# Pooled V by GpSimd and the band mask added in PSUM, from pair 16 on: an hourglass attention with a dense layer behind it

## The chip, the cores and the metric

The kernel runs on one core of a Trainium2 chip. The metric is the device time of one execution in microseconds. The core has five engines that work side by side, each with its own instruction queue: TensorE (PE in the profile) multiplies matrices, VectorE (DVE), ScalarE (ACT) and GpSimd (POOL) work element by element, and SyncE (SP) issues nearly all DMAs here. Sixteen DMA engines move the data. An instruction waits in its queue until what it depends on is done, and everything behind it on that queue waits with it.

## The reference

Two parts follow each other. The first is attention over q, k and v of shape (8, 8, 576, 64): eight batches, eight heads, 576 tokens, 64 channels. Each head is computed twice and the results are added: once on tokens averaged in groups of four (144 of them, the result repeated four times), and once with a band mask that lets a token see only those less than four positions away.

```python
q_d = q.reshape(B, H, Sd, factor, D).mean(axis=3)      # factor = 4, Sd = 144; k_d, v_d likewise
out_up = np.repeat(sm_attn(q_d, k_d, v_d), factor, axis=2)
mask = np.abs(pos[:, None] - pos[None, :]) < factor
scores = np.where(mask, scale * np.matmul(q, k.transpose(0, 1, 3, 2)), -1000000000.0)
out_local = np.matmul(softmax(scores), v)
return out_up + out_local
```

The second part is dense, over x, the attention's result as 4608 tokens of 512 channels, with weights of 512 x 2048 and 2048 x 512:

```python
h = x @ w_in
g = h - np.tanh(h)
return g @ w_out
```

## The kernel before

**Tiling of attention.** Two heads of one batch make a pair; there are 32 pairs, four to a batch, and two pairs make a head block (`hb`). For the band, the 576 tokens are cut into five windows (`NT`) of 128 keys each, 112 apart, so a window's keys stand on the 128 partitions and its 112 or 120 queries on the free dimension. The pooled attention has 144 keys and queries (`G`). They are laid out window by window as well, 32 to a window, 160 columns in all (`GW`), with some groups in two windows.

**One pair, step by step.** SP loads q and k (`qkn`) and v (`vst`, in the window layout) in 64-channel fp32 rows. A cast to bf16 gives `qr` (line 452) and `vw` (line 390). A transpose, on TensorE for the first eight pairs and by DMA after that (line 457), gives channels on partitions, reordered by ScalarE into `qk` (line 465). Two additions (lines 499 and 508) sum each four neighbouring tokens into `qkd`. The scores are written into PSUM: the first four windows by line 517 into one pair of banks, the fifth window and the pooled scores (line 539) into another. From pair 14 on both go in one step, `s12`. ScalarE takes the exponentials into the tile `E`: line 557 the 912 columns of the first four windows, line 569 the 240 of the fifth, line 572 the 640 of the pooled scores. The band mask is then multiplied in: the large mask (912 columns, line 561) on VectorE, the small one (240 columns, line 576) on VectorE or GpSimd. The first four pairs (`BIASED`) instead get a bias from a matmul with the identity ahead of the scores. The output matmuls (lines 585 and 591) multiply `E` with `vw` and with the pooled v, `vd`, each of which has a column of ones (or fours) that gives the softmax sum. VectorE divides (lines 602 and 604) into `ln`. The result is transposed, by TensorE for pairs 0 to 7, 11 and 15 (lines 615 and 618), by a DMA for the other 22 (line 621, tile `lT`), and the pooled part, repeated four times, is added in the join (lines 633 and 637, on GpSimd or VectorE), which writes `xT`, the input of the dense part.

**Pooled v.** `pool_v(hb)` makes `vd` for two pairs at once: four matmuls with 32 columns of a pooling matrix (line 405) and one with 128 (line 407), then a copy out of PSUM (line 412), by ScalarE but for the first head blocks.

**The dense part.** Block `kb` of the dense part covers 512 tokens (even `kb`) or 640 (odd). Line 675 multiplies by `w_in` into PSUM (four matmuls for each of 16 slices of the hidden dimension, twice for an odd block), ScalarE takes tanh (line 686), VectorE subtracts (line 689) into `gT`, and line 711 multiplies by `w_out`. `dense(kb)` interleaves the first product of block `kb` with the second one of block `kb - 1`. Block `kb` can start when the joins of batch `kb` are done.

**The order.** The whole program is written as a list of operations with a duration, the keys they read and write, and a priority; some have alternatives on several engines (`P.choice`). `Program.order` then simulates the engines and issues at each moment the ready operation of lowest priority number. Attention's priorities are ten times the pair's number, the dense matmuls have 5000, so the dense part fills what attention leaves of TensorE. The simulated order is the order in each engine's queue on the chip. DMAs are simulated as one resource with a cost each (`T_QK`, `T_V`, `T_IN`, `T_OUT`), at most eight outstanding from SP. From pair 12 on (`GATE`) the loads of pair `p` wait until pair `p - 5`'s result was sent to its DMA transpose. Loads are issued four pairs ahead: there are four `qkn` and five `vst` buffers.

Of the kernel before, what the change touches and what calls it, by code (L numbers as in the profile page):

```python
# [8 lines left out]
FP32 = mybir.dt.float32  # L9
BF16 = mybir.dt.bfloat16  # L10
# [155 lines left out]
def kernel(  # L166
# [9 lines left out]
    nc = tc.nc  # L176
# [13 lines left out]
    PIECES = [(0, 0, 120), (1, 0, 112), (2, 0, 56), (2, 56, 56), (3, 0, 112), (4, 0, 120)]  # L190
    GW = 32 * NT
    Q0 = [0, 120, 232, 344, 456]
# [18 lines left out]
    bias = fixed("bias", [128, 576], BF16)  # L211
    xT = [fixed(f"xT{j}", [128, NTOK], BF16) for j in range(NP)]
    w_in_sb = fixed("w_in_sb", [128, N_DC, Dff], BF16)
# [136 lines left out]
    def load_v(p):  # L350

        b, j, s = p // NP, p % NP, p % NVST
        for i in range(2):
            queue = nc.scalar if p in V_ACT else nc.sync

            def issue(i=i, base=v[b, 2 * j + i], queue=queue):
# [4 lines left out]
                 [("sent", p - BEHIND)] if p in GATE else [])  # L361

    def load_w(src, dst, name, f, stage, keys):
# [32 lines left out]
    def pool_v(hb):  # L396

        w = hb % NVW
        pri = 20 * hb - 1
        bank, keys = (ps_ox1, ["ox1"]) if MERGE[2 * hb] else (ps_ox, ["ox"])  # L400
        pv = bank[:, 0, :].rearrange("p (w c) -> p w c", w=2)
# [17 lines left out]
    def attention(p):  # L419
# [7 lines left out]
        cold = 1.1 if p < NP else 1.0  # L427
        biased = p < BIASED


# [71 lines left out]
        def add2(eng):  # L502
            with nc.allow_low_precision("pooled q and k"):
                out = qkd[s].rearrange("p i (t r) -> p i t r", t=NT)
# [3 lines left out]
                eng.tensor_tensor(out=out, in0=a, in1=c, op=ALU.add)  # L508
# [20 lines left out]
        def s2(bank=ps):  # L529
# [6 lines left out]
            for i in range(2):  # L536
                for hh in range(2):
                    rows = slice(64 * hh, 64 * hh + 64)
                    T.matmul(bank[:, hh, 120 + GW * i:120 + GW * i + GW],  # L539
                             qkd[s][rows, 1, 32 * i:32 * i + 128],  # L540
                             qkd[s][rows, 0], start=True, stop=True)

# [13 lines left out]
        e3 = E[s][:, 1152:1792].rearrange("p (h c) -> p h c", h=2)  # L556
        op("ACT", 820, lambda: A.activation(  # L557
            out=e1, in_=ps[:, :, 0:456], func=AF.Exp, scale=SCALE),
           reads=ts, writes=[("E", s, 0)], pri=pri)
        if not biased:  # L560
            P.choice([(eng, ns, lambda fn=fn: fn(  # L561
# [4 lines left out]
        if not merged:  # L566
# [5 lines left out]
        op("ACT", 590, lambda: A.activation(  # L572
            out=e3, in_=ps2[:, :, 120:120 + 2 * GW], func=AF.Exp, scale=SCALE / 16.0),
           reads=ts2, writes=[("E", s, 2)], pri=pri)
        if not biased:
            P.choice([(eng, ns, lambda fn=fn: fn(  # L576
                out=e2v, in0=e2v, in1=mask[:, 456:576].unsqueeze(1).to_broadcast([128, 2, 120]),
                op=ALU.mult)) for eng, ns, fn in MASK2[p >= SMALL]],
                reads=["mask"], writes=[("E", s, 1)], pri=pri)

        def outs():
            for hh in range(2):
# [4 lines left out]
                for half in range(2):  # L587
                    c = 1152 + 2 * GW * hh + 128 * half
# [9 lines left out]
        op("PE", 590 * cold, outs,  # L598
           reads=[("E", s, 0), ("E", s, 1), ("E", s, 2), ("vw", w, jj), ("vd", w)],
           writes=ox, pri=pri)  # L600
# [19 lines left out]
        if XOUT[p] == 'dma':  # L620
# [7 lines left out]
            def join(eng):  # L628
                x = xT[j][:, b * S:(b + 1) * S]
                x0, p0 = (bass.AP(tensor=a.tensor, offset=a.offset,  # L630
                                  ap=[a.ap[0], [n, 2], [1, m]])
                          for a, n, m in ((x, 456, 120), (pool, 130, 30)))
                eng.tensor_tensor(
# [5 lines left out]
                    in0=lT[s][:, 1:4, 0:112].rearrange("p t (g a) -> p t g a", a=4),  # L639
                    in1=pool[:, 32:128].rearrange("p (t g) -> p t g", t=3)[:, :, 2:30]  # L640
                    .unsqueeze(3).to_broadcast([128, 3, 28, 4]), op=ALU.add)
# [93 lines left out]
    def dense(kb):  # L735
# [6 lines left out]
        for _, second, i in steps:  # L742
            if second:
                mm2(kb - 1, i)
            else:
# [155 lines left out]
```

## Time and profile before

| | us |
| --- | --- |
| Median of 3 runs | 327.32 (327.27 to 329.07) |
| The profiled execution, its own time | 327.29 |
| Its span, first to last instruction | 325.6 |

The span's 1.7 us of difference to the execution's time lie around it. The profile names instructions by engine, line of the kernel, and output and input tiles; a group's line gives the count, the busy time, the mean of one, and the idle time of the engine ahead of it with what ended it. In the windows, each engine's busy time in a stretch stands with the number of its instructions; after them the granted TensorE clock, the mean busy share of the sixteen DMA engines (packets overlap, so it can exceed 1) and GB/s. PEld is the loading of weights, which overlaps the matmuls.

### The profile page before, as it was taken

The page shows a single profiled execution, that of the slowest core. Times are in us where ns is not written, and L with a number is a line of the kernel's source. Part 1 is how long each engine was busy: PE and PEld are TensorE (multiplying, and loading weights), DVE is VectorE, ACT ScalarE, POOL GpSimd, SP SyncE. Part 2 cuts the span into 40 slices and gives each one's busy share as a digit, 9 for nine tenths or more (in the row PEclk, how much of TensorE's full clock was granted, in tenths as well). Part 3 has the DMA queues.
Part 4 walks back from the last instruction along what each step waited for, and adds up shares of the span by engine and source line. Part 5 has one row for each costly group of instructions (what it writes and reads, how often), then busy time and mean ns, then how long its engine had stood idle before and what let it go on. Part 6 is the DMA issues. An engine that isn't in the chain of part 4 may idle for free.

```text
span 325.6 us, 7167 instructions
## 1 busy us (share of the span) xinstructions
PE 313.9 (96%) x2643; PEld 175.5 (54%) x2686; DVE 212.5 (65%) x388; ACT 224.7 (69%) x390; POOL 165.6 (51%) x230
## 2 busy tenths in 40 slices
PE   6899999999899999999999999999999999999996
PEld 2565555666544445666654444656554445566544
DVE  6898985789966576765867576778665444554311
ACT  3765987599888969799986978798973444544300
POOL 5688758265846767677767767877440000000000
PEclk9999999999999999999999999999999999999999
DMA  7999999899987999699999999995322001000022
GB/s 205 316 393 367 372 315 273 216 259 217 240 254 106 254 201 294 92 234 219 191 233 165 261 209 263 222 229 106 85 66 62 32 32 67 32 34 32 32 84 81
DMA packets 109715, 59.79 MB, mean 184 GB/s; under 512 B 92656, under 2 KB 92912, under 8 KB 109680
## 3 DMA queue, kind: packets, MB, share of 16 engines
q1 hardware_dynamic: 109680, 59.33, 72.9%
q8 instruction: 21, 0.34, 0.5%
q14 instruction: 14, 0.11, 0.1%
HBM read 37.75 MB, written 9.44 MB: 145 GB/s over the span
## 4 chain that ended last, share of the span: by engine, by line
PE 90%; DVE 4%; issue 2%; POOL 1%; DMA 1%; ACT 1%; SPq 0%; POOLq 0%
PE ps_hy L711 38%; PE ps_hy L675 36%; PE ps_ox L517 3%; PE ps_ox L585 3%; PE ps_ox L591 2%; PE ps_ox L539 1%; PE ps_ox L405 1%; PE ps_ox L618 1%; PE ps_ox L407 1%; DVE ln L604 1%; DVE gT L689 1%; DMA qkn<-in_k_dram 1%; PE ps_ox L615 1%; PE ps_ox L482 1%; PE ps_ts L482 1%
## 5 line engine op out<-in xcount | busy, mean ns | idle before, releaser
L675 PE MATMUL ps_hy<-xT,w_in_sb 128*128 128x320 bf16 (+1 forms) x759 | 146.9, 325 | 1.7 <-DVE gT L689 1.0
L711 PE MATMUL ps_hy<-w_out_sb,gT 128*128 128x512 bf16 (+1 forms) x559 | 139.0, 373 | 2.2 <-issue 1.0
L689 DVE TENSOR_TENSOR gT<-ps_hy,u 128x320 bf16<-128x320 f32 (+1 forms) x192 | 103.2, 553 | 56.0 <-ACT u L686 53.1
L686 ACT ACTIVATE u<-ps_hy 128x320 f32<-128x320 f32 (+1 forms) x192 | 93.6, 497 | 53.2 <-PE ps_hy L675 47.3
L675 PEld LDWEIGHTS <-w_in_sb 128*128 128x128 bf16 x768 | 71.8, 98 | 53.4 <-issue 1.7
L711 PEld LDWEIGHTS <-gT 128*128 128x128 bf16 x592 | 56.0, 98 | 52.8
L499 POOL TENSOR_TENSOR half<-qk 128x576 f32<-128x576 bf16 x29 | 33.3, 1148 | 48.7 <-ACT qk L465 33.9
L465 ACT COPY qk<-qT 128x576 bf16<-128x576 bf16 x44 | 52.3, 1207 | 0.0
L452 POOL CAST qr<-qkn 128x576 bf16<-128x576 f32 x48 | 33.4, 707 | 13.0 <-DMA qkn<-in_k_dram 6.2
L604 DVE TENSOR_TENSOR ln<-ps_ox,r 128x896 bf16<-128x896 f32 x32 | 34.9, 1091 | 1.1
L561 DVE TENSOR_TENSOR E<-E,mask 128x912 bf16<-128x912 bf16 x28 | 24.0, 856 | 10.4 <-ACT E L557 10.4
L557 ACT ACTIVATE E<-ps_ox 128x912 bf16<-128x912 f32 x28 | 26.2, 937 | 4.9 <-PE ps_ox L517 4.6
L726 DVE COPY y<-ps_hy 128x512 f32<-128x512 f32 (+1 forms) x21 | 13.9, 663 | 20.2 <-PE ps_hy L711 19.1
L390 POOL CAST vw<-vst 128x640 bf16<-128x640 f32 x32 | 25.5, 796 | 2.4 <-DMA vst<-in_v_dram 2.3
L508 POOL TENSOR_TENSOR qkd<-half 128x320 bf16<-128x320 f32 x29 | 23.9, 823 | 1.8 <-DVE r L602 1.1
L572 ACT ACTIVATE E<-ps_ox 128x640 bf16<-128x640 f32 x28 | 20.0, 716 | 0.0
L585 PE MATMUL ps_ox<-vw,E 128*128 128x65 bf16 x320 | 19.3, 194 | 0.4 <-ACT vd L412 0.3
L585 PEld LDWEIGHTS <-E 128*128 128x128 bf16 x320 | 16.4, 98 | 5.7 <-issue 0.3
L576 POOL TENSOR_TENSOR E<-E,mask 128x240 bf16<-128x240 bf16 x18 | 13.6, 756 | 9.4 <-ACT E L569 9.3
L591 PE MATMUL ps_ox<-vd,E 128*128 128x65 bf16 x256 | 18.0, 193 | 0.1
L517 PEld LDWEIGHTS <-qk 64*128 64x128 bf16 x320 | 9.2, 95 | 16.1 <-issue 12.5
L602 DVE RECIPROCAL r<-ps_ox 128x14 f32<-128x14 f32 x32 | 7.7, 242 | 14.3 <-PE ps_ox L591 12.4
(78 smaller groups left out, 240.2 us busy)
## 6 DMA issues: line engine op xcount, KB each, us to landing
vst<-in_v_dram SPq DMA_DIRECT2D x64, 160.0 KB, 4.2
qkn<-in_q_dram SPq DMA_DIRECT2D x32, 288.0 KB, 4.1
qkn<-in_k_dram SPq DMA_DIRECT2D x32, 288.0 KB, 4.1
out_dram<-y SPq DMA_DIRECT2D x35, 256.0 KB, 2.5
gT<-in_moe_w_in_dram SPq DMA_DIRECT2D x4, 1024.0 KB, 8.1
xT<-in_moe_w_out_dram SPq DMA_DIRECT2D x8, 256.0 KB, 5.2
gT<-in_moe_w_out_dram SPq DMA_DIRECT2D x2, 1024.0 KB, 10.2
qT<-qr SPq DMA_TRANSPOSE x24, 4.2
```

The source lines that it names most:

```text
L390: P.choice([(eng, ns, lambda fn=fn: fn(out=vw[w][:, 2 * jj:2 * jj + 2, :, 0:64], in_=vst[s])) for eng, ns, fn in CAST_V[p >= NEARLY]], rea ...
L452: P.choice([(eng, ns, lambda dst=dst, srt=srt, fn=fn: fn(out=dst, in_=srt)) for eng, ns, fn in (any3[2:] if p >= CASTS else any3[:1] + any ...
L465: fn(out=full[:, i].rearrange("p (g a) -> p g a", a=A9), in_=qT[s][:, :, i::2].rearrange("p a g -> p g a"))
L499: eng.tensor_tensor(out=half, in0=four[:, :, :, 0:2], in1=four[:, :, :, 2:4], op=ALU.add)
L557: op("ACT", 820, lambda: A.activation(out=e1, in_=ps[:, :, 0:456], func=AF.Exp, scale=SCALE), reads=ts, writes=[("E", s, 0)], pri=pri)
L585: T.matmul(po[:, hh, 65 * t:65 * t + 65], E[s][:, c:c + 128], vw[w][:, 2 * jj + hh, t, :], start=True, stop=True)
L591: T.matmul(po[:, hh, o:o + 65], E[s][:, c + GW * i:c + GW * i + 128], vd[w][:, i, 2 * jj + hh, :], start=(i == 0), stop=(i == 1))
L604: op("DVE", 1010, lambda: V.tensor_tensor(out=ln[s].rearrange("p n (h d) -> p h n d", d=D), in0=blocks[:, :, :, 0:64], in1=r[s].unsqueeze( ...
L675: T.matmul(ps_hy[slot][:, 0:n], w_in_sb[:, dc, fc * 128:(fc + 1) * 128], xT[dc][:, t0 + c0:t0 + c0 + n], start=(dc == 0), stop=(dc == N_DC ...
L686: op("ACT", 90 + 76 * n // 100, lambda: A.activation(out=u[us][:, 0:n], in_=ps_hy[slot][:, 0:n], func=AF.Tanh), reads=[("hy", slot)], writ ...
L689: op("DVE", 70 + 105 * n // 100, lambda: V.tensor_tensor(out=gT[g][:, fc, c0:c0 + n], in0=ps_hy[slot][:, 0:n], in1=u[us][:, 0:n], op=ALU.s ...
L711: T.matmul(ps_hy[slot][:, 0:c1 - c0], gT[g][:, fc, ts * 128:ts * 128 + 128], w_out_sb[:, fc, c0:c1], start=(fc == 0), stop=(fc == N_FF - 1))
```

## The change

From pair 16 on (`DIRECT`), the pooled v of a pair no longer comes from `pool_v`. SP loads v a second time, in rows of four tokens (256 fp32 values) onto 72 partitions, two rows of each head to a partition (`load_pool`), into one of two buffers in the part of `xT` that belongs to batches 0 and 1. GpSimd sums the four tokens in two additions (`sum_v`). The pooled scores of these pairs use 144 columns in place of 160, and two tiles of 72 pooled keys in place of two of 128. Also from pair 16 on (`FORE`), VectorE adds the bias to the scores in PSUM ahead of the exponential, and the multiplication by the large mask behind it goes; the small mask stays a multiplication, on GpSimd only. From pair 8 on (`SMALL`, 12 before) the planner may put the small mask on GpSimd. Some durations that the planner is given change too.

```diff
-    xT = [fixed(f"xT{j}", [128, NTOK], BF16) for j in range(NP)]
+    xall = fixed("xT", [128, NP, NTOK], BF16)
+    xT = [xall[:, j] for j in range(NP)]
...
+    def load_pool(p):
+        b, j, n = p // NP, p % NP, p % 2
+        base = v[b, 2 * j]
+        def issue():
+            nc.sync.dma_start(out=vp(n), in_=bass.AP(
+                tensor=base.tensor, offset=base.offset,
+                ap=[[4 * D, KP], [KP * 4 * D, 4], [1, 4 * D]]))
+        load(650, issue, [("vp", n)] + [("x", c, i) for c in range(2) for i in range(NP)] * (p < DIRECT + 2),
+             T_P, -30 + 0.06 + 0.1 * p, behind=[("sent", p - BEHIND)])
+    def vp(n):
+        return xall[0:KP, :, 512 * n:512 * n + 512].bitcast(FP32)
+    def sum_v(p):
+        n, w, jj = p % 2, (p // 2) % NVW, p % 2
+        first = p < DIRECT + 2 * NVW
+        t = vp(n)
...
+        def add1(eng):
+            eng.tensor_tensor(out=t[:, :, 0:128], in0=t[:, :, 0:128],
+                              in1=t[:, :, 128:256], op=ALU.add)
+        def add2(eng):
+            with nc.allow_low_precision("pooled v"):
+                eng.tensor_tensor(out=vd[w][0:KP, jj, :, 0:64],
+                                  in0=t[:, :, 0:64], in1=t[:, :, 64:128], op=ALU.add)
+        for n1, fn, to in ((1030, add1, ("vp", n)), (630, add2, ("vdd", w, jj))):
+            P.choice([("POOL", n1, lambda fn=fn: fn(GP))],
+                     reads=[("vp", n)] + [("vd", w)] * first, writes=[to], pri=10 * p - 8)
...
+        if 2 * hb >= DIRECT:
+            return
...
-                    T.matmul(bank[:, hh, 120 + GW * i:120 + GW * i + GW],
-                             qkd[s][rows, 1, 32 * i:32 * i + 128],
-                             qkd[s][rows, 0], start=True, stop=True)
+                    k0 = (KP if direct else 32) * i
+                    T.matmul(bank[0:kp, hh, 120 + gw * i:120 + gw * i + gw],
+                             qkd[s][rows, 1, k0:k0 + kp],
+                             qkd[s][rows, 0, 0:gw], start=True, stop=True)
...
+        def add_bias(bank, part):
+            V.tensor_tensor(out=bank, in0=bank, op=ALU.add, in1=bias[:, part].unsqueeze(1)
+                            .to_broadcast([128, 2, part.stop - part.start]))
+        if p >= FORE:
+            op("DVE", 1025, lambda: add_bias(ps[:, :, 0:456], slice(0, 456)),
+               reads=["bias"], writes=ts, pri=pri)
...
-        if not biased:
+        if BIASED <= p < FORE:
...
-                op=ALU.mult)) for eng, ns, fn in MASK2[p >= SMALL]],
+                op=ALU.mult)) for eng, ns, fn in MASK2[p >= SMALL][p >= FORE:]],
...
-                                 E[s][:, c + GW * i:c + GW * i + 128],
+                                 E[s][0:kp, c + gw * i:c + gw * i + 128],
+                                 vd[w][0:kp, jj, 2 * hh + i, :] if direct else
...
+    FORE = 16
...
+    DIRECT, T_P = 16, 860
...
-    SMALL = 12
+    SMALL = 8
...
-    MASK1 = [[("DVE", 700, V.tensor_tensor)]] * 2
-    MASK2 = [[("DVE", 300, V.tensor_tensor)], [("DVE", 300, V.tensor_tensor), ("POOL", 700, GP.tensor_tensor)]]
+    MASK1 = [[("DVE", 760, V.tensor_tensor)]] * 2
+    MASK2 = [[("DVE", 300, V.tensor_tensor)], [("DVE", 300, V.tensor_tensor), ("POOL", 630, GP.tensor_tensor)]]
...
-    POOL_V = [("POOL", 670, GP.tensor_copy)]
+    POOL_V = [("POOL", 690, GP.tensor_copy)]
...
-            ("POOL", 610, GP.tensor_copy)]
+            ("POOL", 630, GP.tensor_copy)]
...
-    ADDERS = [[("DVE", 760, 450, V), ("POOL", 1100, 670, GP)],
-              [("POOL", 1100, 670, GP)]]
+    ADDERS = [[("DVE", 760, 450, V), ("POOL", 1120, 690, GP)],
+              [("POOL", 1120, 690, GP)]]
...
+            if nl[0] >= DIRECT:
+                load_pool(nl[0])
...
+            if p + 2 >= DIRECT:
+                sum_v(p + 2)
```

More of the change, by code (lines that the diff above doesn't have):

```diff
@@ L190 @@
     PIECES = [(0, 0, 120), (1, 0, 112), (2, 0, 56), (2, 56, 56), (3, 0, 112), (4, 0, 120)]
-    GW = 32 * NT
+    GW, KP = 32 * NT, G // 2
     Q0 = [0, 120, 232, 344, 456]
@@ L361, in load_v @@
                  [("sent", p - BEHIND)] if p in GATE else [])
+    def load_pool(p):
[13 more added lines that the diff above has]
+        t = vp(n)
+        if first:
+            op("DVE", 70, lambda: V.memset(vd[w][0:KP, jj, :, 64:65], 4.0),
+               writes=[("vd", w)], pri=10 * p - 12)
+        def add1(eng):
[8 more added lines that the diff above has]
+                     reads=[("vp", n)] + [("vd", w)] * first, writes=[to], pri=10 * p - 8)
     def load_w(src, dst, name, f, stage, keys):
@@ L428, in attention @@
         biased = p < BIASED
+        direct = p >= DIRECT
+        gw, kp = (G, KP) if direct else (GW, 128)
         yield
@@ L503, in add2 @@
             with nc.allow_low_precision("pooled q and k"):
+                if direct:
+                    eng.tensor_tensor(out=qkd[s][:, :, 0:G], in0=half[:, :, :, 0],
+                                      in1=half[:, :, :, 1], op=ALU.add)
+                    return
                 out = qkd[s].rearrange("p i (t r) -> p i t r", t=NT)
@@ L555, in attention @@
         e2v = E[s][:, 912:1152].rearrange("p (h c) -> p h c", h=2)
-        e3 = E[s][:, 1152:1792].rearrange("p (h c) -> p h c", h=2)
+        e3 = E[s][0:kp, 1152:1152 + 4 * gw].rearrange("p (h c) -> p h c", h=2)
+        def add_bias(bank, part):
[4 more added lines that the diff above has]
+               reads=["bias"], writes=ts, pri=pri)
         op("ACT", 820, lambda: A.activation(
@@ L572, in attention @@
         op("ACT", 590, lambda: A.activation(
-            out=e3, in_=ps2[:, :, 120:120 + 2 * GW], func=AF.Exp, scale=SCALE / 16.0),
+            out=e3, in_=ps2[0:kp, :, 120:120 + 2 * gw], func=AF.Exp, scale=SCALE / 16.0),
            reads=ts2, writes=[("E", s, 2)], pri=pri)
@@ L587, in outs @@
                 for half in range(2):
-                    c = 1152 + 2 * GW * hh + 128 * half
+                    c = 1152 + 2 * gw * hh + 128 * half
                     o = 65 * (NT + half)
@@ L598, in attention @@
         op("PE", 590 * cold, outs,
-           reads=[("E", s, 0), ("E", s, 1), ("E", s, 2), ("vw", w, jj), ("vd", w)],
+           reads=[("E", s, 0), ("E", s, 1), ("E", s, 2), ("vw", w, jj), ("vd", w)] +
+           [("vdd", w, jj)] * direct,
            writes=ox, pri=pri)
@@ L631, in join @@
                                   ap=[a.ap[0], [n, 2], [1, m]])
-                          for a, n, m in ((x, 456, 120), (pool, 130, 30)))
+                          for a, n, m in ((x, 456, 120), (pool, 114 if direct else 130, 30)))
                 eng.tensor_tensor(
@@ L639, in join @@
                     in0=lT[s][:, 1:4, 0:112].rearrange("p t (g a) -> p t g a", a=4),
-                    in1=pool[:, 32:128].rearrange("p (t g) -> p t g", t=3)[:, :, 2:30]
+                    in1=(pool[:, 30:114].rearrange("p (t g) -> p t g", t=3) if direct else
+                         pool[:, 32:128].rearrange("p (t g) -> p t g", t=3)[:, :, 2:30])
                     .unsqueeze(3).to_broadcast([128, 3, 28, 4]), op=ALU.add)
```

## The prediction, made before the changed kernel ran

> **What bounds the kernel now.** I read the page first, then the stages.
>
> ```profile
> span 325.6 us, 7167 instructions
> PE 313.9 (96%) x2643; PEld 175.5 (54%) x2686; DVE 212.5 (65%) x388; ACT 224.7 (69%) x390; POOL 165.6 (51%) x230
> ...
> PE   6899999999899999999999999999999999999996
> ...
> POOL 5688758265846767677767767877440000000000
> PEclk9999999999999999999999999999999999999999
> DMA  7999999899987999699999999995322001000022
> ...
> PE 90%; DVE 4%; issue 2%; POOL 1%; DMA 1%; ACT 1%; SPq 0%; POOLq 0%
> ```
>
> TensorE is busy in every slice but the first two and the last, at full granted clock, and the chain that ended last is 90% TensorE. The second thing to see is that the DMA engines are as full as TensorE for two thirds of the span, and empty in the last third. The windows split this by stage:
>
> ```profile
> core 0: us, PE busy (x) PEld busy (x) DVE busy (x) ACT busy (x) POOL busy (x), PEclk, DMA share, GB/s
> 0.00:27.00 27.00, 22.58 (x269) 13.34 (x272) 21.01 (x56) 14.16 (x22) 18.30 (x37) 1.00 0.97 310
> 110.00:220.00 110.00, 108.59 (x968) 60.45 (x985) 75.45 (x126) 91.63 (x151) 81.07 (x107) 1.00 1.02 217
> 247.00:325.60 78.60, 75.09 (x406) 40.26 (x411) 32.08 (x59) 26.86 (x55) 0.00 (x0) 1.00 0.14 50
> ```
>
> From 27 us on TensorE leaves almost nothing: attention's matmuls go first and dense ones fill in. So time can be won only by taking work off TensorE (or its few gaps), and lost only where attention becomes so late that the dense matmuls run out. Attention's own pace (pairs 16 to 31 lie mostly in the second row) has the DMA engines at a share of 1.02, ScalarE at 83%, GpSimd at 74%.
>
> ```profile
> 20.00:30.00 10.00, 9.43 (x117) 5.71 (x117) 8.46 (x13) 4.61 (x9) 8.66 (x15) 1.00 1.08 382
> 80.00:90.00 10.00, 9.12 (x110) 5.96 (x109) 9.89 (x20) 8.80 (x20) 7.50 (x11) 1.00 1.09 231
> 250.00:260.00 10.00, 9.95 (x47) 4.53 (x47) 4.19 (x7) 3.38 (x6) 0.00 (x0) 1.00 0.14 52
> ```
>
> The last row gives the price of a dense matmul of 512 columns: 47 in 10 us, 213 ns each, back to back.
>
> **The change, part by part.** First, pooling V on TensorE goes for head blocks 8 to 15.
>
> ```profile
> 152.29 0.81 PE L711 MATMUL ps_hy<-w_out_sb,gT 128*128 128x512 bf16 x3
> 153.03 0.29 PE L405 MATMUL ps_ox<-vw,pick 128*32 128x256 bf16 x4
> 153.26 0.29 PE L407 MATMUL ps_ox<-vw,pick 128*128 128x256 bf16 x1
> 153.38 1.25 PE L675 MATMUL ps_hy<-xT,w_in_sb 128*128 128x320 bf16 x8
> ```
>
> Three dense matmuls from 152.29 at 213 ns would hand over at 152.93; the next dense one starts at 153.38. The block costs 0.45 us: 0.35 in its five matmuls and 0.10 at its entry. The 64 matmuls of L405 below are 16 blocks, and eight go: 8 x 0.45 = 3.6 us off a full TensorE.
>
> ```profile
> L405 PE MATMUL ps_ox<-vw,pick 128*32 128x256 bf16 x64 | 4.7, 286 | 0.2 <-DVE xT L647 0.2
> L539 PE MATMUL ps_ox<-qkd 64*128 64x160 bf16 x112 | 8.4, 229 | 0.0
> L412 ACT CAST vd<-ps_ox 128x512 bf16<-128x512 f32 x15 | 8.9, 592 | 3.0 <-PE ps_ox L407 2.9
> L561 DVE TENSOR_TENSOR E<-E,mask 128x912 bf16<-128x912 bf16 x28 | 24.0, 856 | 10.4 <-ACT E L557 10.4
> L604 DVE TENSOR_TENSOR ln<-ps_ox,r 128x896 bf16<-128x896 f32 x32 | 34.9, 1091 | 1.1
> L576 POOL TENSOR_TENSOR E<-E,mask 128x240 bf16<-128x240 bf16 x18 | 13.6, 756 | 9.4 <-ACT E L569 9.3
> L499 POOL TENSOR_TENSOR half<-qk 128x576 f32<-128x576 bf16 x29 | 33.3, 1148 | 48.7 <-ACT qk L465 33.9
> ```
>
> The pooled scores narrow from 160 to 144 columns, four matmuls in each of 16 pairs: 64 x 16 columns at 213/512 ns is 0.4 us, half of that if the two halves of the rows run side by side. I take 0.2. The output matmuls keep their number and 65 columns, so nothing there.
>
> ScalarE loses eight copies of 592 ns and a tenth of its third exponential. It isn't the bound (83%), so this counts nothing, but it pays for what follows.
>
> The large mask becomes an addition in PSUM ahead of the exponential. The nearest row is L604, which also reads 896 fp32 elements from PSUM: 1.09 us, so about 1.1 against 0.86 for L561. On VectorE that is 16 x 0.25 = 4 us more at 69% busy. The chain of a pair stays as long but for that 0.25 us: score, add, exponential in place of score, exponential, mask. What is new is that ScalarE now waits for VectorE, with the tanh of the dense part queued behind it. A VectorE late by one L604 costs ScalarE about 1.1 us, against a spare of 18.4 us over some 14.7 pairs (110 us at about 7.5 a pair), 1.25 us a pair, and the 0.3 just freed. Cost 0; without that cover up to 1.1 us in some pairs. PSUM is held by the scores about 1.3 us longer of 7.5, and its other user there, the V pooling, is gone: 0.
>
> The small masks: 18 of the 20 from pair 12 on are on GpSimd already, so at most two move in the late pairs and four in pairs 8 to 11. Those four matter through the one gap that TensorE has after its start:
>
> ```profile
> 83.58 1.11 PE L675 MATMUL ps_hy<-xT,w_in_sb 128*128 128x320 bf16 x7 [0.78 <-DVE gT L689]
> ```
>
> In 80 to 90 us VectorE is busy 9.89 of 10, and TensorE waits 0.78 us for it. Less on VectorE there should close this: gain 0.8, bounds 0 and 0.8 (a new order of the whole program could also open one like it elsewhere, so 0.8 lost is the far end). The changed costs in the planner move work before pair 16 too; that has no row of its own, and I put it inside the same bound.
>
> GpSimd gets two additions per pair. By L499 (576 elements in 1148 ns, 2.0 ns each) 512 elements are 1.02 us and 256 are 0.5; together 1.5 a pair. It has 81.07/14.7 = 5.5 us of 7.5 now, so 7.0 to 7.2 with its masks: nearly full.
>
> ```profile
> L508 POOL TENSOR_TENSOR qkd<-half x29: 715/721/1208, 16.0 to 237.6; 128x320 bf16<-128x320 f32 x29
> L576 POOL TENSOR_TENSOR E<-E,mask x18: 637/641/1036, 98.1 to 243.3; 128x240 bf16<-128x240 bf16 x18
> ```
>
> ```profile
> 151.86 0.88 DVE L561 TENSOR_TENSOR E<-E,mask 128x912 bf16<-128x912 bf16 x1 [0.92 <-ACT E L557]
> ```
>
> ```profile
> 152.21 1.12 POOL L508 TENSOR_TENSOR qkd<-half 128x320 bf16<-128x320 f32 x1
> ```
>
> GpSimd's operations have a floor and a tail, and the tail case shown, 1.12 against 0.72 us, started under the mask multiplication L561. The Trainium skill, SBUF — State Buffer, section "SBUF: two separate sides", says that a VectorE operation with two SBUF inputs takes the port pair it shares with GpSimd exclusively for the whole instruction. The row agrees; by that rule the addition in PSUM, with one SBUF input, no longer blocks GpSimd, up to 0.4 us a pair back. No run shows it yet, and I leave it out of the sum; it lowers the chance of the GpSimd rival a little.
>
> The new load goes on SP's queue, among the q, k and V loads and both kinds of transposes, and waits for GpSimd to have read its buffer two pairs before. All transposes queue behind that wait.
>
> ```profile
> vst<-in_v_dram SPq DMA_DIRECT2D x64, 160.0 KB, 4.2
> qkn<-in_q_dram SPq DMA_DIRECT2D x32, 288.0 KB, 4.1
> ```
>
> It moves 72 x 4 x 256 fp32, 295 KB a pair, one q load's worth. Full DMA engines moved 382 GB/s at a share of 1.08 in 20 to 30 us (large pieces) and 217 at 1.02 in 110 to 220 us: 354 or 213 GB/s, 0.83 or 1.39 us a pair. Its 1 KB rows are nearer to the large pieces; I take 0.9. As the DMA engines are full, attention falls behind by that much a pair. Whether TensorE notices depends on the slack between a batch's last join and the first dense matmul that reads it:
>
> ```profile
> 0.00:163.70 163.70, 0.50 (x1) 6.92 (x9) 1.00 0.97 250
> ...
> 0.00:198.50 198.50, 1.44 (x2) 9.21 (x12) 1.00 0.99 245
> ...
> 0.00:255.00 255.00, 3.41 (x5) 13.05 (x17) 1.00 0.90 221
> ```
>
> ```profile
> 0.00:167.05 167.05, 72.59 (x379) 35.05 (x384) 1.00 0.97 251
> ...
> 0.00:204.01 204.01, 89.24 (x441) 41.09 (x448) 1.00 0.99 246
> ...
> 0.00:242.70 242.70, 110.41 (x569) 53.02 (x576) 1.00 0.93 228
> 242.70:273.50 30.80, 16.32 (x62) 6.20 (x64) 1.00 0.18 55
> ```
>
> The first fence counts joins (L637): 10, 14 and 22, with the ten pairs that TensorE turns back these are batches up to 4, 5 and 7. The second counts the weight loads of L675: even blocks have 64, odd ones 128, so 384, 448 and 640 end dense blocks 3, 4 and 6. Slack: 3.4 us for batch 4, 5.5 for batch 5, 18.5 for batch 7. The lateness would be 4 x 0.9 = 3.6, 8 x 0.9 = 7.2 and 14.4. When batch 5 is late, 16 matmuls of the dense block before it (4 x 4 x 213 ns = 3.4 us) can still go first, while a pair moved past that point takes its own matmuls away as cover (ten of about 115 columns, four of 144 and 18 of 65, 2,900 columns, 1.2 us at the same pace). So 7.2 + 1.2 - 5.5 - 3.4 is about zero, and 1.2 with half of the 16. I take 0.7 us lost.
>
> Sum: -3.6 - 0.2 - 0.8 + 0.7 = -3.9 us: a span of 321.7. The execution of that profile took 327.29, 1.7 beside its span, and the median shown is 327.32; so 323.4, say 323.5 us.
>
> **The rivals.** *The load is spread thin, slower than before.* It covers 72 partitions where the others cover 64 or 128. 72 does not split evenly over 16 engines as 64 and 128 do; over 12 it would, six partitions each, and those 12 would become the bound. Then the slow price is 1.39 x 16/12 = 1.85 us a pair. Batch 7 is then 16 x 1.85 = 29.6 late against 18.5 + 3.4, and some 2 us of cover are gone: 10 us idle, 327.3 - 4.6 + 10 = 332.7. It decides from 1.25 us a pair on (18.5 + 3.4 - 2 over 16 pairs; at batch 5 the first idle time comes at 0.96) and eats the whole gain at about 1.55. For it: the share of 1.02. Against it: each pair's loads start some four pairs ahead, and only slow pricing reaches it. The Trainium skill, DMA: Bandwidth & Descriptors, section "Why a DMA increments its semaphore by 16 and not by 1", gives the rule: the largest number up to 16 that divides the slowest dimension, here 12. No row shows a load of 72 partitions. With my 0.9 it would be 1.2 a pair: 9.6 + 1.2 - 5.5 - 3.4 = 1.9 idle, 327.3 - 4.6 + 1.9 = 324.6.
>
> *GpSimd becomes late, no change.* At 7.2 of 7.5 us an operation with the tail of L576 (0.4 us) in half to all of 16 pairs makes TensorE's output matmuls wait in order: 3 to 6 us, 326 to 329. For it: TensorE's order is fixed beforehand, so any lateness is a gap. Against it: the pace has slack as above, and the shared-port tail may shrink.
>
> *The order is only reshuffled.* If the gap at 83 us stays and the wait for batch 5 is 1.2, the sum is -2.6; with another gap of that size it is -1.8: 324.7 to 325.5. For it: every duration that the planner is given on GpSimd changes. Against it: the slack between attention and the dense blocks absorbs most of a changed order.
>
> **How the numbers follow.** One per cent, 3.3 us, is about what a measurement tells from no change: faster is below 324.0, slower above 330.6. Forecast with its gain kept, 0.50; the reshuffle and the milder DMA wait (324 to 326), 0.18; GpSimd late, 0.14; load spread thin, 0.18, nearly all of it above 330.6. The range starts at 321.5 (no wait at all and 1 us more off the start, where TensorE is busy 22.58 of 27) and reaches 331, which leaves most of the slow case out.
>
> **What would show it.** Right: L405 x32 in place of x64; TensorE's idle time as small as before from 27 us; no gap in 80 to 90 us; the PSUM addition near 1.1 us; GpSimd above 90% in 120 to 230 us; the end of attention some 10 us later with the dense blocks not waiting. Wrong: gaps of TensorE ahead of L675 that a join released (DMA), or ahead of L585 and L591 that GpSimd released; a landing of the new load far above 4.2 us; SP's queue waiting for GpSimd.

## The result, and the profile after

The changed kernel took 407.79 us (median of 6 runs, 403.88 to 411.50), the kernel before, run beside it, 327.35: a ratio of 1.243 (95% interval 1.237 to 1.249). The prediction was 323.5 us, with a range from 321.5 to 331.

The page of the changed kernel, with its busy times, TensorE's slices and granted clock, and the chain that ended last:

```profile
span 407.1 us, 7182 instructions
PE 343.7 (84%) x2648; PEld 182.3 (45%) x2648; DVE 219.0 (54%) x398; ACT 218.8 (54%) x380; POOL 187.0 (46%) x260
...
PE   6899999997958879566866795669768999999996
...
PEclk9999999999879989888789898979679999999999
...
PE 68%; DMA 13%; issue 7%; POOL 5%; DVE 5%; ACT 2%; SPq 1%; POOLq 0%; ACTq 0%
PE ps_hy L731 30%; PE ps_hy L767 28%; DMA xT<-in_v_dram 12%; PE ps_ox L563 2%; POOL xT L390 2%; PE ps_ox L638 2%; PE ps_ox L644 1%; DVE ln L659 1%; DMA qkn<-in_k_dram 1%; PE ps_ox L673 1%; PE ps_ox L586 1%; PE ps_ox L670 1%; DVE gT L745 1%; PE ps_ox L524 1%; POOL qr L494 1%
```

The lines have moved: L731 is what L675 was (the first dense product, reading `xT`), L767 what L711 was. All of TensorE's slices but the first two and the last were full before; now there are holes from about 100 to 310 us, which is the stretch in which the second load runs. Two numbers carry the whole loss. TensorE's idle time (span less busy) went from 11.7 to 63.4 us, 51.7 more; its busy time went from 313.9 to 343.7, 29.8 more, though it has fewer columns to compute. Together that is the 81.5 us by which the span grew.

The new name on the chain is `xT<-in_v_dram`, the second load of V. The list of waits, sorted by total (who waited, for whom, us in total, times, longest), says who stood still for it:

```profile
PE ps_hy L731 <- DMA xT<-in_v_dram: 46.9, 16, 4.7
...
POOL xT L390 <- PE ps_hy L731: 38.5, 13, 5.3
```

```profile
SPq L370 <- PE ps_hy L731: 29.4, 8, 8.6
```

The dense matmuls wait for the load 16 times, once for each pair that has one. The sum on GpSimd (L390) waits for dense matmuls, and SP's issue of the load (L370, the last fence, from SP's own list) waits for dense matmuls too. None of the three has a reason in the data: the load fills tokens that belong to batches 0 and 1, and the dense matmuls of that time read batch 2 and later. One such wait in the timelines of SP and of TensorE:

```profile
113.12 1.05 SPq L370 DMA_DIRECT2D xT<-in_v_dram  x1
```

```profile
118.34 1.86 PE L731 MATMUL ps_hy<-xT,w_in_sb 128*128 128x512 bf16 x4 [4.68 <-DMA xT<-in_v_dram]
120.00 3.36 PE L767 MATMUL ps_hy<-w_out_sb,gT 128*128 128x512 bf16 x8
123.20 1.03 PE L731 MATMUL ps_hy<-xT,w_in_sb 128*128 128x512 bf16 x4
124.06 0.59 PE L767 MATMUL ps_hy<-w_out_sb,gT 128*128 128x512 bf16 x2
```

SP issues the load at 113.12; TensorE stands still for 4.68 us until it has landed. What follows shows the other part of the loss: the twelve matmuls from 118.34 to 123.20 take 0.40 us each, those from 123.20 on 0.215. The windows of the same kernel give the granted clock beside it:

```profile
core 0: us, PE busy (x) PEld busy (x) DVE busy (x) ACT busy (x) POOL busy (x), PEclk, DMA share, GB/s
...
110.00:120.00 10.00, 5.32 (x42) 2.41 (x41) 3.21 (x7) 5.46 (x8) 7.64 (x10) 0.81 1.04 212
120.00:130.00 10.00, 9.70 (x65) 4.21 (x63) 4.52 (x9) 6.23 (x10) 4.26 (x5) 0.85 0.58 154
130.00:140.00 10.00, 8.34 (x66) 4.12 (x67) 5.34 (x9) 6.24 (x10) 5.30 (x9) 1.00 0.74 190
```

The clock was 0.81 and 0.85 in these two windows and 1.00 in the next. Over the span its mean is 0.924: 0.076 of 407.1 us is 30.9 us, close to the 29.8 us by which TensorE's busy time grew.

### The profile page after: what moved, and what is told of

It is laid out like the page before. It is cut to its first block, busy times and chain, and to the rows that moved or that the text cites. A ratio compares the mean times of both kernels' runs of the same rounds, so it can differ in the third digit from the quotient of the medians.

```text
span 407.1 us, 7182 instructions
## 1 busy us (share of the span) xinstructions
PE 343.7 (84%) x2648; PEld 182.3 (45%) x2648; DVE 219.0 (54%) x398; ACT 218.8 (54%) x380; POOL 187.0 (46%) x260
## 4 chain that ended last, share of the span: by engine, by line
PE 68%; DMA 13%; issue 7%; POOL 5%; DVE 5%; ACT 2%; SPq 1%; POOLq 0%; ACTq 0%
PE ps_hy L731 30%; PE ps_hy L767 28%; DMA xT<-in_v_dram 12%; PE ps_ox L563 2%; POOL xT L390 2%; PE ps_ox L638 2%; PE ps_ox L644 1%; DVE ln L659 1%; DMA qkn<-in_k_dram 1%; PE ps_ox L673 1%; PE ps_ox L586 1%; PE ps_ox L670 1%; DVE gT L745 1%; PE ps_ox L524 1%; POOL qr L494 1%
## 5 line engine op out<-in xcount | busy, mean ns | idle before, releaser
L731 PE MATMUL ps_hy<-xT,w_in_sb 128*128 128x320 bf16 (+1 forms) x768 | 160.7, 344 | 55.1 <-DMA xT<-in_v_dram 46.9
L767 PE MATMUL ps_hy<-w_out_sb,gT 128*128 128x512 bf16 (+1 forms) x592 | 156.3, 395 | 0.0
L731 PEld LDWEIGHTS <-w_in_sb 128*128 128x128 bf16 x768 | 73.8, 101 | 119.5 <-issue 44.7
L767 PEld LDWEIGHTS <-gT 128*128 128x128 bf16 x592 | 58.7, 102 | 60.1 <-issue 11.3
L390 POOL TENSOR_TENSOR xT<-xT 72x512 f32<-72x512 f32 x16 | 20.2, 1264 | 38.6 <-PE ps_hy L731 38.5
L428 POOL CAST vw<-vst 128x640 bf16<-128x640 f32 x32 | 23.6, 738 | 1.8 <-DMA vst<-in_v_dram 1.8
L605 DVE TENSOR_TENSOR ps_ox<-ps_ox,bias 128x912 f32<-128x912 f32 x16 | 17.8, 1113 | 8.4 <-PE ps_ox L563 8.1
L625 ACT ACTIVATE E<-ps_ox 72x576 bf16<-72x576 f32 (+1 forms) x28 | 18.8, 670 | 0.0
L644 PE MATMUL ps_ox<-vd,E 128*128 128x65 bf16 (+1 forms) x256 | 18.5, 195 | 0.1
L563 PE MATMUL ps_ox<-qk 64*128 64x120 bf16 (+1 forms) x280 | 15.1, 231 | 0.0
```

The lines of the kernel that those rows point to most:

```text
L390: eng.tensor_tensor(out=t[:, :, 0:128], in0=t[:, :, 0:128], in1=t[:, :, 128:256], op=ALU.add)
L563: T.matmul(out, qk[s][rows, 1, KW * t:KW * t + 128], qk[s][rows, 0, Q0[t]:Q0[t] + NQ[t]], start=not biased, stop=not biased or t >= 3)
L731: T.matmul(ps_hy[slot][:, 0:n], w_in_sb[:, dc, fc * 128:(fc + 1) * 128], xT[dc][:, t0 + c0:t0 + c0 + n], start=(dc == 0), stop=(dc == N_DC ...
L767: T.matmul(ps_hy[slot][:, 0:c1 - c0], gT[g][:, fc, ts * 128:ts * 128 + 128], w_out_sb[:, fc, c0:c1], start=(fc == 0), stop=(fc == N_FF - 1))
```

## The experiments

**Is it the buffer?** The first theory (A): the buffer `vp(n)` is one access over four planes of `xT`, 512 columns out of each 4608, and the layer that gives the instructions their semaphores takes all that lies between its first and last byte as touched. Then every dense matmul and join in between is ordered against the load. The rivals were those that the prediction had named: DMA engines too full, and GpSimd overrun. `own` changes nothing but where the buffer lies; the order in each engine's queue stays that of the changed kernel.

```diff
-    xall = fixed("xT", [128, NP, NTOK], BF16)
-    xT = [xall[:, j] for j in range(NP)]
+    xT = [fixed(f"xT{j}", [128, NTOK], BF16) for j in range(NP)]
+    vps = fixed("vp", [128, 4, 256], FP32, 2)
...
-        return xall[0:KP, :, 512 * n:512 * n + 512].bitcast(FP32)
+        return vps[n][0:KP]
```

> The second load of V gets two buffers of its own; xT is four tiles again; the order of every queue is that of the changed kernel. Theory A (the load and the sums touch four planes of xT in one strided access, and its whole extent is taken as touched, so dense matmuls and joins are made to wait for the load and the load for them, though no byte is shared): the waits of the dense matmuls on that load go, TensorE's granted clock is 1.00 again, 322 to 327 us. Rival B (the DMA engines are too full for 16 more loads): lateness stays whatever the buffer is, 350 us or more. Rival C (GpSimd is overrun by the sums): 330 to 345 us, with gaps of TensorE ahead of the output matmuls.

Measured: 326.18 us, ratio 0.997 (0.995 to 0.999), clock 1.00.

```profile
span 325.7 us, 7165 instructions
PE 315.1 (97%) x2648; PEld 175.1 (54%) x2648; DVE 223.6 (69%) x398; ACT 217.3 (67%) x380; POOL 188.6 (58%) x260
...
PEclk9999999999999999999999999999999999999999
```

81 us went with the buffer. Both kernels have the same 2648 matmuls, so here the loss can be parted: TensorE's idle time is 10.6 us in place of 63.4, its busy time 315.1 in place of 343.7. The DMA engines and GpSimd have the same work here as in the changed kernel, so whatever they cost lies within these 326.18 us.

`halves` keeps the one tile `xT` and the load in it, but gives each head's part one contiguous piece of one plane: two DMAs and twice two sums for a pair.

```diff
-            nc.sync.dma_start(out=vp(n), in_=bass.AP(
+            for e in range(2):
+                nc.sync.dma_start(out=vp(n, e), in_=bass.AP(
...
-        return xall[0:KP, :, 512 * n:512 * n + 512].bitcast(FP32)
+        return xall[0:KP, 2 * n + e, 0:1024].bitcast(FP32).rearrange("p (i c) -> p i c", c=256)
```

> One tile xT as in the changed kernel, and the second load of V in it, but as two DMAs, each into one contiguous piece of one plane (1024 tokens' room for one head), and the sums in two pieces each. Theory A (it is the extent of the strided access, not the shared tile): no dense matmul waits for the load, 323 to 330 us, a little over the kernel with own buffers for GpSimd's two more instructions a pair. Rival (sharing one tile with xT is enough): 380 us or more, as in the changed kernel.

Measured: 328.00 us, ratio 1.001 (1.000 to 1.002), clock 1.00. So it was the access across planes that made the waits. Sharing a tile with `xT` costs none of the 80 us; `halves` is 1.8 us over `own`, and its shared tile and its two more sums a pair are not parted. That whole extents are counted is the reading that fits; the rule itself was not tested.

`shared_half_dose` is the changed kernel with the load from pair 24 on (`DIRECT = 24`).

> The changed kernel with its strided buffer in xT, but the second load and the sums only from pair 24 (the mask in PSUM from pair 16 as before). Theory A (each load makes the dense matmuls wait once): half of the loss, 362 to 373 us, eight waits of dense matmuls for the load instead of 16. Rival (a fixed cost of the shared tile, or the lateness of a saturated DMA): under 340 or over 390 us.

Measured, one run: 361.36 us, 33.8 over before in place of 80.4, a little under the half and the range that were expected.

```profile
PE ps_hy L731 <- DMA xT<-in_v_dram: 17.4, 6, 4.4
PE ps_hy L731 <- POOL xT L390: 4.5, 5, 1.4
```

Six waits are put down to the load and five to its sum on GpSimd. The loss follows the number of loads, if not exactly.

**How much is the clock?** `shared_fillers` puts twelve matmuls of constants ahead of the dense group behind each load, 15 of 16 times. They write into the bank that this group overwrites.

```diff
+            held_back.append(p)
...
         def mm(dcs):
+            if held_back:
+                held_back.clear()
+                for _ in range(FILL if dcs[0] == 0 else 0):
+                    T.matmul(ps_hy[slot], ident, mask[:, 0:512], start=True, stop=True)
```

> The changed kernel with its strided buffer, and 12 matmuls of constants (512 columns, 2.6 us at full clock, into the bank that the next dense group overwrites) ahead of the dense group that follows each load, 15 of 16 times. Theory (the gaps cost about 50 us by themselves and some 30 us more because TensorE's granted clock is halved for 3.4 to 6.8 us behind each gap of over 2.3 us; the fillers lie in the gaps and keep the clock up): 375 to 388 us, mean granted clock above 0.97. Rival (the clock is not set by the gaps): 404 us or more, clock still near 0.92.

Measured, one run: 391.85 us, 16 less than the changed kernel's median (12 less than its fastest run), and 4 over the expected range. Most of the fast clock came back:

```profile
core 0: 390.1 us, clock 0.987
```

0.013 of 390.1 us is 5.1 us lost to the clock in place of 30.9. Of the 25.8 us won, 16 reached the time: the fillers are 180 x 213 ns = 38 us, longer than some gaps and not in all of them. So some 16 of the 80 us at least were the clock's, at most the 30 of the busy time. That the gaps set the clock holds; the gain was expected too high.

**What the parts are worth once the buffer is right.** `own` saves 1.5 us by the medians where 3.9 were predicted. `mask_only` is the changed kernel without the second load (`DIRECT = 32`), `own_no_psum_mask` is `own` with the mask multiplied in all pairs (`FORE = 32`).

> The changed kernel without the second load: all pairs pool V on TensorE, with the mask in PSUM from pair 16, the small masks from pair 8 and the new planner costs; xT is one tile. Theory A: the one tile costs nothing, the mask in PSUM about nothing, the gap near 83 us closes: 326 to 328 us. Rival (ScalarE, waiting for VectorE's addition, holds back the tanh of the dense part): 331 us or more, with ScalarE's waits on the addition in the list.

> Own buffers for the second load, and the large mask multiplied behind the exponential in all pairs. Theory A (the gain is the eight V poolings off TensorE, 3.6 us): 322 to 326 us, within 1 us of the kernel with own buffers. Rival (the addition in PSUM gives GpSimd its time back, since the mask multiplication blocks it): 2 us or more over the kernel with own buffers, GpSimd's pooled-q-and-k addition with a longer mean than with own buffers alone.

Measured: `mask_only` 328.57 us, ratio 1.003 (1.002 to 1.004); `own_no_psum_mask` 326.76, ratio 0.997 (0.995 to 0.999). The mask in PSUM without the load wins nothing, as the theory had it, though the time is a little over its range. With it or without it `own` is the same, 0.6 us apart, both above the 326 us that the theory allowed the second; yet GpSimd's pooled-q-and-k addition does differ between the two, as the rival said (the first fence is `own_no_psum_mask`, the second `own`):

```profile
L547 POOL TENSOR_TENSOR qkd<-half 128x288 bf16<-128x288 f32 x16 | 12.6, 787 | 0.2
```

```profile
L547 POOL TENSOR_TENSOR qkd<-half 128x288 bf16<-128x288 f32 x16 | 10.6, 665 | 0.1
```

The mean is 787 ns with the mask multiplication on VectorE and 665 without it. That this is the multiplication's doing is not shown: in two kernels of this section the same addition takes 738 ns without it (`own_new_costs`) and 696 with it (`own_old_no_psum_mask`). It is time of an engine that TensorE doesn't wait for here.

Where the rest of `own`'s gain goes can be sought in TensorE's timeline (the profiled execution of `own` took 327.47 us, 1.3 over its median, so it shows more loss than most): the first dense matmul in the kernel before (first fence) and in `own` (second), and one output block of `own`, with VectorE beside it in the last fence.

```profile
22.74 0.38 PE L675 MATMUL ps_hy<-xT,w_in_sb 128*128 128x512 bf16 x1
```

```profile
23.80 0.59 PE L731 MATMUL ps_hy<-xT,w_in_sb 128*128 128x512 bf16 x2
...
124.15 0.30 PE L638 MATMUL ps_ox<-vw,E 128*128 128x65 bf16 x4 [0.46 <-DVE E L614]
125.42 0.20 PE L638 MATMUL ps_ox<-vw,E 128*128 128x65 bf16 x1 [0.97 <-DVE E L629]
```

```profile
121.32 2.78 DVE L614 TENSOR_TENSOR E<-E,mask 128x912 bf16<-128x912 bf16 x1
124.02 1.34 DVE L629 TENSOR_TENSOR E<-E,mask 128x240 bf16<-128x240 bf16 x1
```

The dense part starts 1.06 us later, in a stretch of the program where neither the load nor the mask has begun. And the masks of pair 15, still multiplied, take 2.78 and 1.34 us on VectorE (the first has a median of 0.83 in the kernel before), so the output matmuls wait 1.4 us. `own_old_costs` keeps `own`'s buffers, the load, the sums and the mask in PSUM, and gives the planner back its durations of before, with small masks from pair 12.

```diff
-    SMALL = 8
+    SMALL = 12
...
-    MASK1 = [[("DVE", 760, V.tensor_tensor)]] * 2
+    MASK1 = [[("DVE", 700, V.tensor_tensor)]] * 2
...
-    ADDERS = [[("DVE", 760, 450, V), ("POOL", 1120, 690, GP)],
-              [("POOL", 1120, 690, GP)]]
+    ADDERS = [[("DVE", 760, 450, V), ("POOL", 1100, 670, GP)],
+              [("POOL", 1100, 670, GP)]]
```

> Own buffers, with the second load, the sums and the mask in PSUM, but the planner's durations of before and the small masks on GpSimd from pair 12 as before. Theory (with own buffers the 3.6 us of V pooling are saved, and are given back by the new order: the dense part starts 1.1 us later, one output block near 124 us waits 1.8 us for VectorE's masks, some 0.9 us go at 60 and 85 us): 322.5 to 324.5 us. Rival (the gain is given back by the load and the sums themselves, whatever the order): 326 to 328 us.

Measured: 324.01 us, ratio 0.989 (0.987 to 0.992), the fastest of all. `own_new_costs` and `own_small_from_8` part the two things that it takes back.

> Own buffers and the planner's new durations, small masks on GpSimd from pair 12 as before. Theory (the new durations reorder the program's start, so the dense part begins 1.1 us later, and leave the masks of pair 15 on a VectorE that GpSimd slows): 325.5 to 327 us, the dense part's first matmul near 23.9 us. Rival (it is the small masks from pair 8 that gave the gain back): 323.5 to 324.5 us.

> Own buffers and the planner's durations of before, small masks on GpSimd from pair 8. Theory (the durations did it): 323.5 to 324.5 us, the first dense matmul near 22.9 us, the gap near 83 us open or closed. Rival (the small masks did it): 325.5 to 327 us.

Measured: `own_new_costs` 327.44 us, ratio 0.998 (0.996 to 1.000), and its first dense matmul is at 24.99 us (first fence); `own_small_from_8` 324.43 us, ratio 0.991 (0.989 to 0.993), and its first dense matmul is at 22.83 (second).

```profile
24.99 0.38 PE L731 MATMUL ps_hy<-xT,w_in_sb 128*128 128x512 bf16 x1
```

```profile
22.83 0.38 PE L731 MATMUL ps_hy<-xT,w_in_sb 128*128 128x512 bf16 x1
```

It was the durations: the four runs of `own_small_from_8` (324.13 to 325.49) and the ten of `own_new_costs` (326.16 to 327.82) don't overlap, though the second kernel is a little over its range. How they cost it is only half shown. In the trace of `own_new_costs` no output matmul waits for the masks of pair 15, which was half of the theory. And the start of the dense part depends on more than the order: `mask_only`, with the new durations and the same 230 matmuls in the same order ahead of it as `own`, starts it at 22.46 us. The same three matmuls, early in the program, in `own_new_costs`, `own` and `mask_only`:

```profile
9.95 1.46 PE L931 MATMUL ps_ts<-lT 128*128 128x512 bf16 x3
```

```profile
9.16 1.02 PE L931 MATMUL ps_ts<-lT 128*128 128x512 bf16 x3
```

```profile
7.80 0.82 PE L931 MATMUL ps_ts<-lT 128*128 128x512 bf16 x3
...
22.46 0.59 PE L731 MATMUL ps_hy<-xT,w_in_sb 128*128 128x512 bf16 x2
```

They take 1.46, 1.02 and 0.82 us: in the first execution TensorE still ran at its slow pace, in the last already at its fast one, though the clock row of all three pages shows full clock there. From these matmuls on `mask_only` is 1.36 us ahead of `own`, and 1.34 at the first dense one. In the kernel before they take 1.06 us, much as in `own`, so the late start of `own` is not of this kind. But some of the 24.99 is the moment at which the clock rose in that execution, and the medians, not the start, carry the verdict. Most of the new durations are nearer to the trace's means, and the order that they make is worse. `own_old_sums` asks whether true durations of the new sums help.

> Own buffers, the durations of before and small masks from pair 12, but the two sums of V given to the planner at 1230 and 700 ns, near what they take, in place of 1030 and 630. Theory (TensorE has no idle time left behind the first 27 us but the gap near 83 us, so a truer plan wins nothing): 323.5 to 324.6 us. Rival (a true duration of GpSimd's work lets attention run closer): 323.4 us or less.

Measured: 325.35 us, ratio 0.994 (0.991 to 0.997), 1.3 us over `own_old_costs`, 0.7 over the expected range: a truer plan won nothing and lost a little.

`own_old_no_psum_mask` is `own_old_costs` with the mask multiplied in all pairs.

> The same with the large mask multiplied behind the exponential in all pairs. Theory (the mask's place is worth little while TensorE has other work): within 1 us of the kernel with own buffers and the old durations. Rival (the multiplication and GpSimd block each other, and GpSimd is nearly full): 2 us or more over it, with the mean of the mask multiplication above 1 us.

Measured: 330.50 us, ratio 1.011 (1.005 to 1.016). Here the rival is right by its time and its mean, 6.5 us over `own_old_costs`. The multiplication's group, and TensorE's waits (the profiled execution took 334.0 us, the slowest of the four; the others took 329.6 to 330.6):

```profile
L614 DVE TENSOR_TENSOR E<-E,mask 128x912 bf16<-128x912 bf16 x28 | 28.6, 1022 | 13.9 <-ACT E L610 13.8
```

```profile
PE ps_hy L767 <- DVE gT L745: 1.8, 2, 1.4
PE ps_ox L638 <- DVE E L629: 1.6, 1, 1.6
...
PE ps_ox L638 <- DVE E L614: 1.3, 1, 1.3
```

It takes 1022 ns in the mean, against 856 in the kernel before, where GpSimd has no sums of V. But the mean hides what happened. Shortest, median and longest in `own_old_no_psum_mask` (with the longest one itself) and in `own_no_psum_mask`, which has the same sums:

```profile
L614 DVE TENSOR_TENSOR E<-E,mask x28: 623/754/4409, 33.8 to 257.9; 128x912 bf16<-128x912 bf16 x28
...
186.87 4.41 DVE L614 TENSOR_TENSOR E<-E,mask 128x912 bf16<-128x912 bf16 x1 [0.39 <-ACT E L610]
```

```profile
L614 DVE TENSOR_TENSOR E<-E,mask x28: 621/762/2132, 33.8 to 247.8; 128x912 bf16<-128x912 bf16 x28
```

Both medians are below the 830 of the kernel before. It is single multiplications that take long; the one of 4.41 us, with the small mask behind it, is what TensorE's two waits for E (1.3 and 1.6 us) are for. With the new durations the mean is 827 and the time no worse (`own_no_psum_mask`), so a fuller GpSimd alone doesn't explain the loss, and how much of the 6.5 us the long ones make in the three faster runs is not shown. So the mask's place in PSUM is worth between nothing and 6.5 us, by the order around it.

## Why the prediction was wrong

**The step that failed** is the sentence on the new load: it "waits for GpSimd to have read its buffer two pairs before". That was taken from the keys in the list of operations. The instructions' real waits come from the addresses that each of them touches, and the diff's first lines had made one tile of four and laid a strided buffer into it. The prediction priced the load's issue, its bytes and its wait on SP, and never asked who else touches the buffer's tile. What the runs showed in its place: 16 waits of the dense matmuls for a load that shares no data with them, 46.9 us, and a clock that fell after them; with a buffer of its own the kernel takes 326.18 us in place of 407.79. No rival has it either: the slower one was the same load, priced as bytes, at 332.7 us. The part "what would show it" did name the sign, gaps of TensorE ahead of the dense product, but expected a late join behind them.

**The V pooling, -3.6 us.** Right in kind; its size was not measured by itself. With the own buffer and the durations of before, 324.01 us are 3.6 under the 327.61 of the kernel before in the same session, but all the other terms are in that, and with the same durations and the mask multiplied the kernel was 2.9 over. That the sum meets the term so closely is in part luck. `mask_only` and `own`, which differ in the pooling, what comes with it and the tile, are 2.4 us apart. TensorE is full again in `own_old_costs` (its slices, from that kernel's page):

```profile
PE   6899999999899999999999999999999999999996
```

**The narrower pooled scores, -0.2.** In TensorE's timeline of `own` the block of the pooled scores takes 221 ns in place of 234, but the output block 577 in place of 561 (medians), which the prediction had at nothing: over 16 pairs -0.2 and +0.3.

**The gap near 83 us, -0.8.** Not won in any kernel with a net effect. In `own` and `mask_only` two waits, of 0.63 and about 0.25 us, stand in its place. In `own_old_costs` it is there as before:

```profile
83.80 1.25 PE L731 MATMUL ps_hy<-xT,w_in_sb 128*128 128x320 bf16 x8 [0.78 <-DVE gT L745]
```

In `own_small_from_8`, where the masks of pairs 8 to 11 may go to GpSimd, it is gone and two others stand in TensorE's timeline, the far end that the prediction had named for this term:

```profile
32.63 0.56 PE L524 MATMUL ps_ox<-ident,qr 128*128 128x128 bf16 x7 [0.62 <-ACT u L742]
...
203.79 1.11 PE L731 MATMUL ps_hy<-xT,w_in_sb 128*128 128x320 bf16 x7 [0.77 <-POOL xT L692]
```

**The addition in PSUM.** Its duration was forecast at 1.1 us. The changed kernel's groups have it, and the sums below it:

```profile
L390 POOL TENSOR_TENSOR xT<-xT 72x512 f32<-72x512 f32 x16 | 20.2, 1264 | 38.6 <-PE ps_hy L731 38.5
...
L605 DVE TENSOR_TENSOR ps_ox<-ps_ox,bias 128x912 f32<-128x912 f32 x16 | 17.8, 1113 | 8.4 <-PE ps_ox L563 8.1
...
L395 POOL TENSOR_TENSOR vd<-xT 72x256 bf16<-72x256 f32 x16 | 11.6, 728 | 1.4 <-DVE xT L692 0.4
```

1113 ns: right. That ScalarE's wait for it costs nothing held too, in `mask_only` to within 0.3%. What was missed is the other side: leaving the multiplication on VectorE cost 6.5 us in one order, and nothing in another. The Trainium skill, SBUF — State Buffer, section "SBUF: two separate sides", was cited for GpSimd being blocked; its rule is that whichever starts first holds the shared port pair for the whole instruction and the other waits. The 2.78 us of `own`'s mask multiplication, from 121.32 to 124.10, agree with it only in part. GpSimd beside it:

```profile
120.96 0.76 POOL L692 TENSOR_TENSOR xT<-lT 128x336 bf16<-128x336 bf16 x1
121.68 0.66 POOL L547 TENSOR_TENSOR qkd<-half 128x288 bf16<-128x288 f32 x1
122.29 0.66 POOL L494 CAST qr<-qkn 128x576 bf16<-128x576 f32 x1
122.89 0.72 POOL L428 CAST vw<-vst 128x640 bf16<-128x640 f32 x1
```

By the rule it would wait for the first of these, which was running when it started. It ended only after the other three, which started later, had ended too. Why they went ahead of it is not shown.

**GpSimd's sums, 1.5 us a pair.** Under-sized: 1264 and 728 ns, 2.0 us a pair. GpSimd is busy 93.55 of 110 us in `own`, 85%, and in `own_old_costs` 100.24 of the 110 us from 120 on, the sign of over 90% that the prediction had named. TensorE doesn't wait for it there. The row of `own`:

```profile
110.00:220.00 110.00, 108.53 (x936) 60.27 (x934) 83.74 (x136) 85.58 (x143) 93.55 (x123) 1.00 1.10 240
```

**The load's bytes, 0.7 us lost.** The DMA share rose from 1.02 to 1.10 (the row above), but in `own` and `own_old_costs` no dense block waited for a join, so the slack covered it and the 0.7 was not lost. The wait that the prediction worked out, of dense block 5 for the joins of batch 5, is there in `own_small_from_8`: it is the 0.77 us at 203.79 shown above. The rival of a thinly spread load did not come: at 10 us lost it is excluded by `own` and `own_old_costs`. On how many engines the load runs was not measured.

**The reshuffle.** It was a rival at 0.18 and up to 2 us. With the buffer repaired it is what took most of the gain: 2.2 us by the medians of `own_old_costs` and `own`, 3.4 by those of `own_old_costs` and `own_new_costs`, which differ in the durations alone. It came from durations that differ by 20 to 70 ns; by which waits is shown in part only.

## What to carry to other kernels

A buffer laid into a free corner of another tile brings its waits along: before pricing its bytes, list every instruction that touches the tile in that time, and see whether the access is one contiguous piece or a stride across pieces that others use. In the profile the sign is a wait whose two sides share no data. And where an order is planned from durations, compare a change under the old durations first: here the order that new durations made took 2.2 to 3.4 us of a gain of 3.6. And a time early in a profile, or a mean, can be one execution's chance: compare the same instructions, and look at the median and the longest.

## What the hardware showed

The granted clock halves behind short gaps. In the changed kernel's records TensorE's clock went to 0.5 in 13 stretches of 3.4 or 6.8 us, 61 us together, each in or soon after a gap of 2.3 us or more; the windows above show it as 0.81 and 0.85. The length of a gap doesn't decide alone: one of 1.95 us was followed by such a stretch in `shared_fillers`, and gaps of 2.42 and 2.66 us were not in `shared_half_dose`. The Trainium skill, TensorE: Matmul & The Clock Gate, section "Part 1: The HAM clock gate (the "warmup" mystery)", describes a window of 3.4 us that runs freely, and the steps and the scatter agree with it. The Trainium skill's table there has the low clock come after an idle window of about 3.4 us, though; here gaps of 2 to 3 us were enough. In the changed kernel 16 waits of together 47 us cost about 16 to 30 us more in this way, so here a wait of TensorE in the middle of a busy stretch had to be priced at well over its length.
